# The first part's list of steps in another order, with the first step of 31 weight conversions on ScalarE

## The chip, the cores and the metric

The kernel runs on one core of a Trainium2 chip. The metric is the time of one execution on the device in microseconds (us); less is better. Before the change the median of 3 runs is 954.95 us (954.93 to 955.6).

The core's engines are TensorE (PE in the profile; PEld is its weight load), VectorE (DVE), ScalarE (ACT), GpSimd (POOL) and SyncE (SP), which issues all of this kernel's DMAs. Each engine takes its instructions in the order in which the program puts them. Semaphores between the engines follow from the data: an instruction waits for the last writer of what it reads and for the last readers of what it overwrites.

## The reference

Attention over q, k and v (4 batches, 8 heads, 576 positions, 64 channels), and then two pairs of dense layers over the 2304 tokens of 512 channels:

```python
# in each head; scale = 1/8, factor = 4
out_d     = softmax(scale * mean4(q) @ mean4(k).T) @ mean4(v)      # 144 pooled positions
out_local = softmax(mask(|i - j| < 4, scale * q @ k.T)) @ v        # a band of 7 keys
attn      = repeat(out_d, 4) + out_local
x  = attn as (2304, 512)
h  = x @ w_in;   x = (h * sigmoid(1.702 * h)) @ w_out              # first block, d_ff 2048
h  = x @ w_in2;  y = max(0.01 * h, h) @ w_out2                     # second block
```

The weights come as float64 and are turned into float32 pairs on the chip.

## The kernel before, in words

**Attention** is cut into 16 jobs, one for a batch and a pair of heads (128 channels). Job n's steps carry its number: loads q, k, va, vb, vh; sums over four positions Qd, Kd (VectorE), Va0 to Vb1 (POOL); pooled scores Sd (TensorE), their maximum Mxd (VectorE), exponentials Exd (ScalarE), inverse sums Rcd (VectorE), division Mud (POOL), transposes T0, T1 (TensorE) copied out by C0, C1 (ScalarE), and the product Vd copied out by Od. The band's scores S0 and S1 are for one head each; jobs 0 to 3 have the mask added by TensorE and go through M, N (VectorE) and E (ScalarE, one call for each of five slices), jobs 4 to 7 through A0, A1, Mx, Sb, Ex, Sm. Then Rc and Mu (division, POOL), transposes U0, U1 copied out by D0, D1, products Y0, Y1, and X0, X1, which add both results on VectorE and give x.

**The two blocks** run over 5 groups of columns (512, then four of 448 tokens) and 16 slices m of the 2048 hidden channels. A unit is one group and one slice. L is a unit's first product (12 matmuls into a PSUM bank h), M its second (12 matmuls into the four accumulators). In between stand Gt (ScalarE, out of h), Gd (VectorE), Gh (ScalarE, the rounded part) and Gl (POOL, what is left). Units 0 and 1 take their first product in pieces h0, h1 of 128 channels, after xh and xl have split x. The two banks of h are reused in turn, so L of a unit waits for Gd of the unit two before.

**Weights.** Slice m of the first block has two halves: number 2m (for L of unit m) and 2m + 1 (for M of unit m). w.n loads half n, 512 KB, into one of three stage buffers. Six steps convert it (`w_conv`, `w_bits`): wF scales the upper words of the doubles into t (line 175), wL shifts (177), wS adds the sign (180), wB adds the lower bits (184), wH rounds into the matmul's format (ScalarE, line 156) and wO subtracts to get the rest (POOL, line 203). The first four run on VectorE; there are three buffers for t. `copy` (lines 154 to 157) picks the engine of wF, wH and other copies: VectorE's form is on line 157, ScalarE's on line 156.

**The order.** The first part (jobs 0 to 7, the 32 conversions, units 0 to 13 of L and 0 to 11 of M) is written out by hand as the list ORDER, one token a step. The list is walked from left to right and each step's instructions are put at the end of their engines' queues: each engine has the list's order among its own steps, and the list fixes nothing between engines but by the data. `@V`, `@G` and `@A` put a step on VectorE, POOL or ScalarE instead of its usual engine. z tokens are matmuls on a constant, with no use of their result. t.23, t.25 and t.27 begin job 8. After the list a loop does the remaining units, jobs 8 to 15 and the second block's weights.

`w_slot` gives a slice m its space when its first half's conversion begins (line 198). The 16 such spaces are also what jobs 0 to 3 use for their tiles before.

Of the kernel before, what the change touches and what calls it, by code (L numbers as in the profile page):

```python
# [27 lines left out]
def attn_moe_kernel(ctx: ExitStack, tc, qT_d, kT_d, vh_d, vg_d, w1a, w2a, w1b, w2b, outT):  # L28
# [18 lines left out]
    ENGINES = {"V": V, "G": G, "A": nc.scalar}  # L47
    HEAD = 2
    ORDER = """
        q.0 vb.0 k.0 k.1 Qd.0 q.3 Vb0.0 va.0 Kd.0 q.1 Vb1.0 Kd.1 w.0 Qd.3 z3.12 S1.0 Va0.0 k.2 Va1.0  # L50
        Qd.1 vb.3 Sd.0 vb.1 M1.0 va.2 N1.0 va.5 E1.0 Mxd.0 vb.2 z3.3 S0.0 vh.0 Kd.2 Vb0.3 Exd.0 S1.1
        M0.0 q.2 Vb1.3 N0.0 Va0.2@V Vb0.1 E0.0 vh.1 Sd.1 M1.1 Va1.2 Rcd.0 va.3 Vb0.2 N1.1 Mud.0@V
        vb.4 E1.1 Mxd.1 Vb1.1 w.1 z3.2 T1.0 Vb1.2 T0.0 Rc.0 S0.1 Qd.2 Mu.0 C0.0 q.4 C1.0 Va0.3@V
        S1.2 Exd.1 M0.1 va.1 Vb0.4 Va0.5@V U0.0 N0.1 vh.2 M1.2 U1.0 Vb1.4 Rcd.1 D1.0 N1.2 wF.0 z3.2
        Vd.0 D0.0 w.2 Mud.1 E0.1 wF.1 Y1.0 wL.0 wL.1 Va0.1 T1.1 wS.0 Sd.2 k.3 Od.0 Va1.3 C1.1 Rc.1
        Va1.1 X1.0 va.4 S0.2 E1.2 Mu.1 Mxd.2 T0.1 k.4 M0.2 Y0.0 C0.1 N0.2 Qd.4 vh.3 E0.2 U1.1 Kd.3
        Va0.4 z3.1 Vd.1 vh.4 X0.0 U0.1 Va1.4 Exd.2 Rc.2 S0.3 vb.5 Od.1@V Mu.2 wB.0 D0.1 Rcd.2 z3.1
        S1.3 w.3 xh.0 M0.3 Mud.2 wH.0 wS.1 z3.1 Sd.3 D1.1 N0.3 M1.3 xl.0 E0.3 N1.3 wB.1 Y1.1 T0.2
        Vb0.5 X1.1 U1.2 E1.3 U0.2 C0.2@V wO.0 T1.2 Mxd.3 w.4 Y0.1 C1.2 Rc.3 Exd.3 wF.2 z3.1 h0.0
        Mu.3 X0.1 Vd.2 wL.2 D0.2 Rcd.3 wH.1 wS.2 z2.1 Y0.2 Mud.3 D1.2 Od.2 wB.2 xh.1 Y1.2 wO.1 X0.2  # L60
        w.5 wH.2 U0.3 Kd.4 U1.3 T0.3 wO.2 D1.3 X1.2 C0.3 wF.3 z3.1 T1.3 xh.2 wL.3 C1.3 wS.3 z3.1
        h1.0 xl.2@G D0.3 wF.4 Vd.3 wB.3 Y1.3 xl.1 wL.4 w.6 wH.3 Y0.3 Od.3@V wS.4 wO.3 h0.1 wB.4 X0.3
        h0.2 wH.4 wF.5 S0.4 X1.3 wO.4 wL.5 xh.3 S1.4 wS.5 w.7 xl.3 h1.1 wF.6 wL.6 h1.2 wB.5 q.5 h0.3
        wS.6 wH.5 k.5 h1.3 wB.6 Gt.0 wO.5 L.2 A1.4 wH.6 w.8 Gd.0 wO.6 wF.7 Gh.0 wL.7 wS.7 Gl.0 L.3
        A0.4 wB.7 Gt.1 Mx.4 w.9 wH.7 Gd.1 Sb.4 wF.8 Gh.1 M.0 wL.8 wO.7 wS.8 Ex.4 wB.8 Gl.1 Sm.4 w.10
        wH.8 Sd.4 wO.8@V Gt.2 Rc.4 M.1 Qd.5 Mu.4 Gd.2 wF.9 Gh.2 Kd.5 w.11 Gl.2 wL.9 L.4 wF.10 wS.9
        Gt.3 wL.10 wB.9 wS.10 wH.9 S1.5 wB.10 wO.9 w.12 M.2 A1.5 wH.10 Gd.3 wO.10 wF.11 Gh.3 wL.11
        Gl.3@V L.5 wS.11 Gt.4 w.13 Gd.4 wB.11 Gh.4 wF.12 wH.11 Gl.4 Mxd.4 M.3 wL.12 Exd.4 wO.11
        wS.12 w.14 wB.12 Gt.5 Gd.5 wH.12 S0.5 wF.13 Gh.5 wO.12 Rcd.4 U0.4 wL.13 q.6 M.4 A0.5 D0.4
        Mud.4 Mx.5 k.6 wF.14 w.15 Sb.5 wS.13 wB.13 T1.4 Gl.5 L.6 wL.14 C1.4 wS.14 wH.13 Ex.5 wB.14  # L70
        wO.13 Sm.5 wH.14 w.16 M.5 wO.14 Rc.5 Gt.6 wF.15 Gd.6 Mu.5 wL.15 Gh.6 wS.15 Gl.6 T0.4 wB.15
        w.17 Y0.4 C0.4 wF.16 wH.15 wL.16 Vd.4 wS.16 wO.15 L.7 Od.4@V wB.16 Va1.5 Vb1.5@V wH.16 X0.4
        va.6 wO.16@V vb.6 wF.17 Sd.5 Gt.7 w.18 wL.17 U1.4 Mxd.5 M.6 D1.4 Va0.6 Gd.7 Exd.5 Vb0.6 Qd.6
        Gh.7 Kd.6 Gl.7 Y1.4 Rcd.5 w.19 wF.18 S0.6 X1.4 wL.18 Mud.5 S1.6 wS.17 A0.6 M.7 q.7 wB.17
        A1.6 k.7 wH.17 wS.18 wO.17 w.20 Mx.6 T1.5 wB.18 U0.5 Sb.6 C1.5 vh.5 L.8 wF.19 D0.5 wL.19
        wH.18 wS.19 Ex.6 wO.18 wB.19 w.21 Sm.6 T0.5 Gt.8 Y0.5 wF.20 C0.5 wL.20 wH.19 Gd.8 Vd.5 wO.19
        wS.20 L.9 Gh.8 Od.5@V X0.5 w.22 Gl.8 wF.21 wL.21 wB.20 Va1.6 Sd.6 wS.21 Vb1.6 Gt.9 vb.7
        wH.20 va.7 Gd.9 U1.5 M.8 wO.20 Mxd.6 Gh.9 w.23 Kd.7 Exd.6 Gl.9 D1.5@V wB.21 Y1.5 Va0.7@V
        Vb0.7 wH.21 Rcd.6 S0.7 vh.6 X1.5 Mud.6 Rc.6 S1.7 A0.7 w.24 Mu.6 Qd.7 T1.6 M.9 A1.7 C1.6
        wO.21 wF.22 Mx.7 wL.22 Sb.7 wS.22 T0.6 wB.22 U0.6 Ex.7 L.10 wF.23 w.25 D0.6 wL.23 C0.6 Sm.7  # L80
        wH.22 Rc.7 wO.22 wS.23 Y0.6 Gt.10 wB.23 Mu.7 Gd.10 Vd.6 wH.23 w.26 wF.24 L.11 Gh.10 wO.23
        wL.24 Od.6 Vb1.7@V X0.6 wS.24 Gl.10 wB.24 U1.6 wF.25 Va1.7 Sd.7 Gt.11 D1.6@V w.27 wL.25
        wH.24 Gd.11 Y1.6 wO.24 M.10 Mxd.7 Gh.11 vh.7 wS.25 Exd.7 Gl.11 wB.25 Rcd.7 wH.25 w.28 wF.26
        Mud.7 U1.7 wL.26 M.11 D1.7 X1.6 wO.25 wS.26 wB.26 wF.27 wH.26 wL.27 T1.7 wO.26 w.29 wS.27
        T0.7 C1.7 L.12 C0.7 wB.27 wF.28 wH.27 wL.28 wO.27 wS.28 Vd.7 wB.28 Gt.12 w.30 U0.7 wF.29
        L.13 Od.7@V D0.7 Gd.12 wH.28 wL.29 Gh.12 wO.28@V Gl.12 wS.29 wB.29 Y0.7 w.31 Gt.13 wF.30 t.23
        Y1.7 wH.29 wL.30 Gd.13 wO.29 X0.7 Gh.13 wS.30 Gl.13 wB.30 X1.7 wH.30 wF.31 wL.31 wO.30 wS.31
# [834 lines left out]
```

## Time and profile before

| what | value |
|---|---|
| median of 3 runs | 954.95 us |
| the profiled execution | 953.42 us |
| its span, first to last instruction | 951.6 us |
| TensorE busy (share of the span) | 909.0 us (96%) |
| VectorE busy | 449.3 us (47%) |
| POOL busy | 375.6 us (39%) |
| ScalarE busy | 306.8 us (32%) |
| mean granted TensorE clock | 0.985 |

The profiled execution has 1.82 us around its span. Busy shares are means over stages with different limits, so the stretch 0 to 188.3 us, in which the list's VectorE steps run, is read by itself. In the list of groups a group's mean includes what its instructions waited while they were already on the engine.

### The profile page before, as it was taken

Reading aid. Unit: us, or ns where it says so; the run is one execution under the profiler, and the core shown is the slowest. Engines: PE = TensorE matmul, PEld = TensorE weight load, DVE = VectorE, ACT = ScalarE, POOL = GpSimd, SP = SyncE. Lnnn points to the kernel's source line nnn. Section 1 sums busy time; section 2 is a strip of 40 time slices with the busy share of each in tenths; the row PEclk is TensorE's granted clock in tenths of the full one; section 3 lists DMA queues with packets and bytes.
Section 4 is the critical chain, followed back from the end, with each engine's and each line's share of the span. In section 5 each row is a group of like instructions: output and inputs, shape, how many; then the busy total and the mean of one; then the engine's idle time right before and its main releaser. Section 6 shows DMA issues by size and latency. Waiting matters only on the chain.

```text
span 951.6 us, 14188 instructions
## 1 busy us (share of the span) xinstructions
PE 909.0 (96%) x5562; PEld 790.4 (83%) x5562; DVE 449.3 (47%) x748; ACT 306.8 (32%) x676; POOL 375.6 (39%) x350
## 2 busy tenths in 40 slices
...
DVE  5999999955545538988931311121121112112111
...
GB/s 269 125 153 129 111 166 126 114 134 157 127 141 150 140 186 174 231 230 191 220 205 111 155 78 0 1 10 75 1 1 78 1 1 77 1 1 39 1 1 39
DMA packets 51906, 98.67 MB, mean 104 GB/s; under 512 B 11648, under 2 KB 25984, under 8 KB 51840
## 3 DMA queue, kind: packets, MB, share of 16 engines
...
## 4 chain that ended last, share of the span: by engine, by line
PE 82%; DVE 14%; issue 2%; DMA 1%; SPq 1%; ACT 0%; DVEq 0%; ACTq 0%
PE h L734 39%; PE acc L779 39%; DVE t L180 3%; DVE t L177 2%; DVE t L184 2%; DVE t L157 2%; DMA a<-vg 1%; PE av L568 1%; PE avd L509 1%; DVE g L753 1%; PE scd L438 1%; PE sc L355 1%; DVE stat L389 0%; DVE xf L599 0%; DVE P L369 0%
## 5 line engine op out<-in xcount | busy, mean ns | idle before, releaser
L734 PE MATMUL h<-xh,w 128*128 128x448 f32 (+1 forms) x1280 | 402.6, 375 | 5.7 <-POOL w L203 3.0
L779 PE MATMUL acc<-gh,w 128*128 128x448 f32 (+1 forms) x1280 | 399.2, 373 | 0.6 <-DVE g L753 0.6
L764 POOL TENSOR_TENSOR gl<-g,gh 128x448 fp32r<-128x448 f32 (+1 forms) x159 | 190.8, 1200 | 482.5 <-ACT gh L156 471.6
L734 PEld LDWEIGHTS h<-xh,w 128*128 128x128 f32 x1280 | 241.6, 189 | 36.5 <-POOL w L203 3.9
L779 PEld LDWEIGHTS acc<-gh,w 128*128 128x128 f32 x1280 | 241.6, 189 | 28.4 <-ACT g L752 1.8
L734 PE MATMUL h<-xl,w 128*128 128x448 f32 (+1 forms) x640 | 238.2, 372 | 1.3 <-POOL xl L717 1.3
L779 PE MATMUL acc<-gl,w 128*128 128x448 f32 (+1 forms) x640 | 237.9, 372 | 0.2 <-POOL gl L764 0.2
L760 DVE TENSOR_TENSOR g<-g,h 128x448 f32<-128x448 f32 (+1 forms) x80 | 50.7, 634 | 319.3 <-ACT g L759 319.3
L156 ACT ACTIVATE gh<-g 128x448 fp32r<-128x448 f32 (+1 forms) x160 | 94.3, 589 | 126.1 <-DVE g L753 69.3
L734 PEld LDWEIGHTS h<-xl,w 128*128 128x128 f32 x640 | 121.1, 189 | 13.8 <-POOL xl L717 1.8
L779 PEld LDWEIGHTS acc<-gl,w 128*128 128x128 f32 x640 | 120.8, 189 | 13.1 <-POOL gl L764 0.8
L759 ACT ACTIVATE g<-h 128x448 f32<-128x448 f32 (+1 forms) x80 | 44.4, 555 | 224.8 <-PE h L734 224.5
L753 DVE SCALAR_TENSOR_TENSOR g<-g,h 128x448 f32<-128x448 f32 (+1 forms) x80 | 50.5, 631 | 128.7 <-ACT g L752 128.2
L752 ACT ACTIVATE g<-h 128x448 f32<-128x448 f32 (+1 forms) x80 | 44.3, 554 | 162.6 <-PE h L734 149.8
L180 DVE SCALAR_TENSOR_TENSOR t<-s,t 128x512 uint32<-128x512 uint32 x64 | 82.4, 1288 | 1.6
L203 POOL TENSOR_TENSOR w<-t,w 128x512 fp32r<-128x512 f32 x28 | 39.5, 1416 | 34.5 <-ACT w L156 34.5
L184 DVE SCALAR_TENSOR_TENSOR t<-s,t 128x512 uint32<-128x512 uint32 x64 | 51.3, 802 | 1.8
L241 POOL TENSOR_TENSOR w<-b,w 128x1024 fp32r<-128x1024 f32 x16 | 38.4, 2403 | 7.4 <-ACT w L240 7.4
L382 POOL TENSOR_TENSOR P<-P,stat 128x320 f32<-128x320 f32 (+1 forms) x40 | 33.9, 863 | 18.1 <-DVE stat L421 14.1
L177 DVE TENSOR_SCALAR t<-t 128x512 uint32<-128x512 uint32 x64 | 39.9, 625 | 1.7
L157 DVE TENSOR_SCALAR t<-s 128x512 f32<-128x512 f32 x64 | 36.1, 565 | 3.6 <-DMA s<-w1b 2.7
L156 ACT ACTIVATE w<-t 128x512 fp32r<-128x512 f32 x32 | 20.3, 634 | 50.4 <-DVE t L184 50.4
...
## 6 DMA issues: line engine op xcount, KB each, us to landing
s<-w1a SPq DMA_DIRECT2D x16, 512.0 KB, 3.7
s<-w2a SPq DMA_DIRECT2D x16, 512.0 KB, 3.9
s<-w1b SPq DMA_DIRECT2D x16, 512.0 KB, 4.0
s<-w2b SPq DMA_DIRECT2D x16, 512.0 KB, 4.2
...
b<-wd SPq DMA_DIRECT2D x16, 512.0 KB, 3.5
...
```

Of the source, the lines that this page charges most:

```text
L156: return nc.scalar.activation(out=out, in_=in_, func=AF.Copy, scale=scale)
L157: return nc.vector.tensor_scalar(out=out, in0=in_, scalar1=scale, scalar2=None, op0=ALU.mult)
L177: lambda: nc.vector.tensor_scalar(out=b, in0=b, scalar1=3, scalar2=None, op0=ALU.logical_shift_left),
L180: lambda: nc.vector.scalar_tensor_tensor(out=b, in0=bits[:, :, 1], scalar=0x80000000, in1=b, op0=ALU.bitwise_and, op1=ALU.bitwise_or,),
L184: lambda: nc.vector.scalar_tensor_tensor(out=b, in0=bits[:, :, 0], scalar=29, in1=b, op0=ALU.logical_shift_right, op1=ALU.bitwise_or,),
L734: nc.tensor.matmul(h, w[:, kc * P : (kc + 1) * P], xs[kc][part], start=kc == 0 and i == 0, stop=kc == KC - 1 and i == 2,)
L752: lambda: nc.scalar.activation(out=g, in_=h[:, :n], func=AF.Tanh, scale=0.5 * 1.702),
L753: lambda: nc.vector.scalar_tensor_tensor(out=g, in0=g, scalar=1.0, in1=h[:, :n], op0=ALU.add, op1=ALU.mult),
L759: lambda: nc.scalar.activation(out=g, in_=h[:, :n], func=AF.Copy, scale=0.01),
L760: lambda: nc.vector.tensor_tensor(out=g, in0=g, in1=h[:, :n], op=ALU.max),
L764: lambda: on(G).tensor_tensor(out=gl, in0=g, in1=gh.bitcast(F32), op=ALU.subtract),
L779: nc.tensor.matmul(acc[c][:, :n], w[:, cs], g, start=m == 0 and i == 0, stop=m == NM - 1 and i == 2)
```

## The change

ORDER is replaced as a whole. The new list has the same steps but for the z tokens (17 matmuls instead of 26). 31 of the 32 wF steps have `@A`: all but wF.4. Other marks differ: without `@V` now are Va0.2, Va0.3, Va0.5, Va0.7, Mud.0, C0.2, Od.1, Od.3, Od.4, Od.5, Od.7, Vb1.5, Vb1.7, D1.5, D1.6, wO.8, wO.16 and wO.28; with `@V` now are xl.3, Gl.0, Gl.1, Gl.2, Gl.7, wO.12, wO.13, wO.15, wO.17, wO.20, wO.25, Mu.7 and wH.29. The conversions come in the order 4, 0, 6, 1, 2, 3, 5, 8, 16 with 21, 12, 10 with 9, 7, 14, 20 with 18, 11 with 13, 15, 22, 17 with 19, 24, 26, 31, 28, 23, 25 with 30, 27, 29. Since a slice's second half can now come first, `w_slot` is called for whichever comes first. The diff, cut: the beginning of the new list, the stretch before and after M.0, its end, and the condition.

```diff
     ORDER = """
...
+        w.4 wF.4 wL.4 wS.4 wB.4 wH.4 vb.3 Vb0.3 q.0 Qd.0 k.0 Kd.0 z3.5 S0.0 S1.0 M1.0 N1.0 wO.4 E1.0 vb.4 Vb0.4
+        Vb1.4 M0.0 q.1 Qd.1 N0.0 w.0 wF.0@A E0.0 Sd.0 Mxd.0 Exd.0 wL.0 wS.0 vb.1 Vb0.1 k.1 z3.2 S1.1 M1.1 wB.0
...
+        Kd.3 w.5 va.3 w.3 vh.1 wH.6 Od.0 Exd.2 D1.0 C0.1 D1.1 z3.2 Y1.0 X1.0 E1.3 U0.1 D0.1 vh.4 Rcd.2 Va0.1
+        Va1.1 Vd.1 Sd.3 Mxd.3 Qd.5 S1.5 A1.5 Va0.2 E0.3 Rc.3 Va0.4 Mu.2 U0.2 D0.2 wF.2@A wH.1 wL.2 X0.0 wS.2
+        Va1.4 Exd.3 Rcd.3 z2.1 S0.5 A0.5 Mud.4 T0.4 C0.4 wO.6 wB.2 va.5 vb.5 vh.3 vh.2 w.8 Mud.2 T0.2 C0.2 Sb.4
+        Ex.4 Sm.4 Va1.2 T1.4 C1.4 T1.2 C1.2 U1.2 Y0.1 wF.3@A D1.2 Y1.1 Od.1 X1.1 wL.3 xh.0 X0.1 Mu.3 U0.3 D0.3
...
+        h1.2 L.3 h1.3 w.16 wF.16@A wL.16 wH.8 Gd.2 Gh.2 wS.16 wB.16 wB.21 w.12 vh.5 vb.6 wO.8 L.4 Gl.2@V wF.12@A
+        X0.4 w.10 wL.12 wH.21 wO.21 w.9 wH.16 Gt.1 Gd.1 wS.12 wB.12 wO.16 Gh.1 Gl.1@V M.0 M.1 M.2 X1.4 wF.10@A
+        wL.10 wH.12 wF.9@A wL.9 wS.10 wS.9 wB.10 wB.9 Gt.3 Gd.3 wO.12@V Sb.5 wH.10 wO.10 L.5 wH.9 Gh.3 Gl.3@V
+        w.7 wF.7@A wL.7 wS.7 Gt.4 Gd.4 Gh.4 wB.7 wH.7 wO.9 k.6 Kd.6 Gl.4 q.6 Qd.6 w.14 wF.14@A wL.14 S1.6 Gt.5
...
+        D0.6 Gd.12 Gh.12 Va1.6 Vd.6 Od.6 wB.23 Va0.7 wH.23 w.30 vh.6 Y0.6 w.25 X0.6 wO.28 Mu.7@V Gl.12 Y1.6 X1.6
+        M.10 Gt.13 wF.25@A wF.30@A Vb1.7 t.25 wL.25 wL.30 wS.25 Gd.13 U1.7 D1.7 wS.30 wB.25 wB.30 Mud.7 T1.7
+        C1.7 T0.7 U0.7 C0.7 Va1.7 Vd.7 vh.7 D0.7 Y0.7 w.27 w.29 Od.7 X0.7 Y1.7 wO.23 M.11 Gh.13 wH.25 wO.25@V
+        Gl.13 X1.7 wF.27@A wH.30 wL.27 wS.27 wB.27 wF.29@A wL.29 wO.30 wS.29 wB.29 wH.29@V wO.29 wH.27 wO.27
+        t.27
     """
...
         t, fs = w_bits(e, m, i)
-        if i == 0:
+        if (e, m) not in wt:
             w_slot(e, m)
```

## Rows read from the trace of the kernel before

**Rows 1.** The page's 40 slices of the span, VectorE's busy tenths.
```profile
DVE  5999999955545538988931311121121112112111
```
**Rows 2.** Busy time by stretch: us, then each engine's, granted clock, DMA share, GB/s.
```profile
0.00:20.00 20.00, 15.71 (x136) 9.21 (x138) 10.47 (x24) 9.60 (x47) 11.11 (x26) 0.83 0.91 260
...
40.00:188.30 148.30, 119.62 (x946) 90.08 (x945) 144.25 (x223) 56.10 (x128) 84.30 (x64) 0.93 0.42 133
0.00:188.30 188.30, 149.39 (x1286) 109.24 (x1287) 174.48 (x284) 77.06 (x232) 107.77 (x104) 0.93 0.49 150
188.30:951.60 763.30, 759.57 (x4277) 681.18 (x4275) 274.82 (x465) 229.77 (x444) 267.79 (x246) 1.00 0.29 92
```
**Rows 3.** The chain that ended last, 150 to 190 us: start, us, what.
```profile
150.61 0.84 PE av L568 x24
...
152.24 2.95 PE h L734 x12
...
182.85 0.28 DVE x L599
...
183.26 1.34 PE sc L355 x38
184.60 3.90 PE h L734 x12
```
**Rows 4.** Groups by shape, 0 to 188.3 us: busy us, mean ns | idle before.
```profile
L180 DVE SCALAR_TENSOR_TENSOR t<-s,t 128x512 uint32<-128x512 uint32 x32 | 41.3, 1290 | 0.5
L203 POOL TENSOR_TENSOR w<-t,w 128x512 fp32r<-128x512 f32 x28 | 39.5, 1416 | 34.5 <-ACT w L156 34.5
...
L184 DVE SCALAR_TENSOR_TENSOR t<-s,t 128x512 uint32<-128x512 uint32 x32 | 29.2, 911 | 0.7
...
L177 DVE TENSOR_SCALAR t<-t 128x512 uint32<-128x512 uint32 x32 | 23.7, 744 | 0.6
L156 ACT ACTIVATE w<-t 128x512 fp32r<-128x512 f32 x32 | 20.3, 634 | 50.4 <-DVE t L184 50.4
L157 DVE TENSOR_SCALAR t<-s 128x512 f32<-128x512 f32 x32 | 20.1, 630 | 0.0
...
L753 DVE SCALAR_TENSOR_TENSOR g<-g,h 128x512 f32<-128x512 f32 x14 | 9.5, 677 | 0.1
...
L752 ACT ACTIVATE g<-h 128x512 f32<-128x512 f32 x14 | 8.3, 592 | 12.4 <-POOL gl L764 8.7 <-PE h L734 2.0 <-DVE gl L764 1.8
...
L203 DVE TENSOR_TENSOR w<-t,w 128x512 fp32r<-128x512 f32 x4 | 2.7, 685 | 0.7 <-ACT w L156 0.7
```
**Rows 5.** Timeline, 165 to 176 us: conversions one behind the other (start, us).
```profile
168.16 1.30 POOL L203 TENSOR_TENSOR w<-t,w 128x512 fp32r<-128x512 f32 x1 [2.01 <-ACT w L156]
168.25 1.76 DVE L180 SCALAR_TENSOR_TENSOR t<-s,t 128x512 uint32<-128x512 uint32 x1
170.04 0.69 DVE L184 SCALAR_TENSOR_TENSOR t<-s,t 128x512 uint32<-128x512 uint32 x1
170.65 0.42 DVE L157 TENSOR_SCALAR t<-s 128x512 f32<-128x512 f32 x1
...
171.10 0.43 DVE L177 TENSOR_SCALAR t<-t 128x512 uint32<-128x512 uint32 x1
```
**Rows 6.** Timeline, 31 to 39.5 us: one VectorE instruction beside five of POOL.
```profile
32.23 1.26 POOL L382 TENSOR_TENSOR a<-a,stat 128x640 f32<-128x640 f32 x1
32.27 5.76 DVE L180 SCALAR_TENSOR_TENSOR t<-s,t 128x512 uint32<-128x512 uint32 x1
...
36.22 1.25 POOL L203 TENSOR_TENSOR w<-t,w 128x512 fp32r<-128x512 f32 x1
```
**Rows 7.** DMA issues by line: KB each, median us from issue to landing.
```profile
s<-w1a SPq DMA_DIRECT2D x16, 512.0 KB, 3.7
```
**Rows 8.** Timeline, the first 20 us: VectorE's first instruction, first reduction of scores.
```profile
3.77 0.75 DVE L329 TENSOR_REDUCE a<-a 128x144 f32<-128x576 f32 x1 [3.77 <-DMA a<-qT]
...
10.40 0.48 DVE L402 TENSOR_REDUCE stat<-sc 128x5 f32<-128x320 f32 x1
```

More of the change, by code (lines that the diff above doesn't have):

```diff
@@ L49, in attn_moe_kernel @@
     ORDER = """
[L50 to L87, printed above, removed]
@@ L88, in attn_moe_kernel @@
-        t.25 wB.31 wH.31 wO.31@V t.27
+        w.4 wF.4 wL.4 wS.4 wB.4 wH.4 vb.3 Vb0.3 q.0 Qd.0 k.0 Kd.0 z3.5 S0.0 S1.0 M1.0 N1.0 wO.4 E1.0 vb.4 Vb0.4
+        Vb1.4 M0.0 q.1 Qd.1 N0.0 w.0 wF.0@A E0.0 Sd.0 Mxd.0 Exd.0 wL.0 wS.0 vb.1 Vb0.1 k.1 z3.2 S1.1 M1.1 wB.0
+        N1.1 E1.1 S0.1 M0.1 Rcd.0 N0.1 Rc.0 vb.0 va.0 Vb0.0 Vb1.0 Vb1.1 wH.0 Kd.1 z3.4 Sd.1 q.4 Qd.4 q.2 vb.2
+        k.2 S1.2 k.4 S0.4 Mxd.1 E0.1 Rc.1 S1.4 Kd.4 M1.2 A1.4 Vb1.3 Kd.2 Exd.1 Rcd.1 q.3 w.6 wF.6@A N1.2 E1.2
+        w.2 Qd.2 wL.6 S0.2 M0.2 wS.6 N0.2 Va0.0 A0.4 wB.6 z3.1 Sd.4 Mxd.4 z3.2 Sd.2 Qd.3 Mud.0 T1.0 C1.0 T0.0
@@ new lines, in attn_moe_kernel @@
+        k.3 S1.3 E0.2 M1.3 Rc.2 va.4 va.2 va.1 Mu.0 U0.0 D0.0 wO.0 Mud.1 N1.3 C0.0 U1.0 S0.3 Mxd.2 M0.3 Exd.4
+        w.1 Va1.0 Vd.0 wF.1@A wL.1 T1.1 C1.1 Rcd.4 wS.1 T0.1 Mu.1 vh.0 Y0.0 U1.1 k.5 q.5 Vb0.2 Mx.4 wB.1 N0.3
+        Kd.3 w.5 va.3 w.3 vh.1 wH.6 Od.0 Exd.2 D1.0 C0.1 D1.1 z3.2 Y1.0 X1.0 E1.3 U0.1 D0.1 vh.4 Rcd.2 Va0.1
+        Va1.1 Vd.1 Sd.3 Mxd.3 Qd.5 S1.5 A1.5 Va0.2 E0.3 Rc.3 Va0.4 Mu.2 U0.2 D0.2 wF.2@A wH.1 wL.2 X0.0 wS.2
+        Va1.4 Exd.3 Rcd.3 z2.1 S0.5 A0.5 Mud.4 T0.4 C0.4 wO.6 wB.2 va.5 vb.5 vh.3 vh.2 w.8 Mud.2 T0.2 C0.2 Sb.4
@@ new lines, in attn_moe_kernel @@
+        Ex.4 Sm.4 Va1.2 T1.4 C1.4 T1.2 C1.2 U1.2 Y0.1 wF.3@A D1.2 Y1.1 Od.1 X1.1 wL.3 xh.0 X0.1 Mu.3 U0.3 D0.3
+        U1.3 D1.3 Rc.4 Va0.3 Kd.5 wS.3 wO.1 wH.2 Mud.3 T0.3 C0.3 Vb1.2 Vd.2 wF.5@A T1.3 C1.3 Od.2 Vd.4 Y0.2 X0.2
+        Y1.2 X1.2 xl.0 xh.1 Sd.5 wO.2 h1.0 wB.3 Mxd.5 wF.8@A wL.5 wL.8 Y1.3 Va1.3 xh.2 Vd.3 Od.4 Od.3 Y0.3 X0.3
+        h0.0 xl.1 h0.1 wH.3 Exd.5 Mu.4 U0.4 D0.4 U1.4 h1.1 D1.4 Y1.4 Y0.4 wS.5 X1.3 xh.3 wB.5 wH.5 xl.3@V wS.8
+        Rcd.5 wB.8 wO.3 xl.2@G h0.2 h0.3 Gt.0 Gd.0 Mx.5 Gh.0 Gl.0@V Mud.5 w.21 wF.21@A wL.21 wS.21 wO.5 L.2 Gt.2
```

11 lines of the change are left out of this document (added).

## The prediction

> **What bounds the kernel now.** I read the page's slices first, then the busy time by stretch, then the chain of waits, then groups of instructions. In the slices VectorE stands at 9 tenths from the second slice to the eighth and falls to 5 and below after [rows 1]. The stretches give the edge: until 188.3 us VectorE is busy for 174.48 us, and from 40 us on for 144.25 of 148.3 (97%), while ScalarE has 56.1 there and POOL 84.3; after 188.3 TensorE is busy for 759.57 of 763.30 us [rows 2]. So the run is two stages in a row: some 184 us in which VectorE sets the pace, and a dense TensorE stage of fixed length. The seam is on the chain: X1 of job 7 (an addition on VectorE) ends at 183.1, the next scores on TensorE wait for it, and from 184.60 TensorE doesn't stop [rows 3]. What the change is worth is by how much that addition comes earlier. TensorE's work behind it is the same.
>
> In the first stage the 32 weight conversions are the largest item: 0.630 + 0.744 + 1.290 + 0.911 = 3.575 us each on VectorE, 114.4 of the 174.5 us [rows 4]. These means are not the price of the instructions. Left alone, the first two take 0.42 and 0.43 us and the last 0.69; the third took 1.76 where a POOL subtraction of 1.30 had started 0.09 before it, and it ended 0.55 us after that one [rows 5]. At 32.27 the same form took 5.76 us, across several POOL instructions that followed each other from 32.23 to 37.47 [rows 6]. So VectorE waits for POOL in these forms: (0.630-0.42) + (0.744-0.43) + (1.290-0.69) + (0.911-0.69) = 1.34 us a conversion, 43 us in all (the third's undisturbed price is taken as the fourth's, the same form).
>
> **The change, part by part.**
>
> *31 first steps (all but that of conversion 4) go to ScalarE.* VectorE loses between 31 x 0.42 = 13.0 us and 31 x 0.630 = 19.5 us [rows 4, 5]. I take 13.0: POOL's subtractions are still there, and what the first step waited for them the second will likely wait for.
> The Trainium skill (SBUF - State Buffer, Who interferes with whom) says that a VectorE instruction in a two-port mode or with two SBUF inputs and a GpSimd instruction exclude each other for a whole instruction, and that ScalarE waits for nobody. The row of 5.76 us agrees. By that rule the saving is the undisturbed price, 13.0 us, and not the mean's 19.5.
>
> ScalarE gains 31 steps. It doesn't show this form; its nearest row, the rounding copy of the same tile, takes 0.634 us [rows 4], so some 19.7 us on top of 77 in 188 [rows 2]: half used. Its price lies between VectorE's undisturbed 0.42 (13 us) and, for the wider stride of the doubles' upper words, twice the row (1.27, 39 us); I take the row. Even the upper end leaves ScalarE under 120 of some 170 us, so its sum doesn't bind; its order may, which is the next term.
>
> *The wait it adds.* VectorE's second step now waits for ScalarE, whose queue is in order: ahead of the first step stand wH of earlier conversions, Gt (waits for TensorE) and Gh. Behind the waiting wL stand all of VectorE's steps. I walked one stretch by rows, each step starting when its engine and its inputs are free: 0.43 or 0.69 for VectorE's conversion steps [rows 5], 0.68 for Gd, wO and Gl there, 0.63 for ScalarE's copies and wF, 0.59 for Gt [rows 4]. Numbers are ends, with Gd.1's end as 0. VectorE: wS.12 0.69, wB.12 1.38, Gl.1 2.06, X1.4 2.4; ScalarE: Gh.1 0.63, wF.10 1.26, wH.12 (after wB.12) 2.01, wF.9 2.64. VectorE: wL.10 2.83, wL.9 3.26, then wS.10, wS.9, wB.10, wB.9 to 6.0; ScalarE: Gt.3 3.2. Gd.3 6.7, wO.12 7.4; ScalarE wH.10 5.9, wH.9 6.6, Gh.3 7.3, wF.7 8.0; VectorE Gl.3 8.1, wL.7 next. No stall, without POOL's delays, which give ScalarE more room. Likewise wF.14 is done at 11.9 where VectorE wants it at 12.0. Where Gt waits for TensorE (Gt.0, Gt.1) I find 0.3 to 0.5 us. A slot of the three stage buffers is refilled as soon as wB has read it, and a load lands 3.7 us after its issue [rows 7]; the tightest pair (wB.16 to wF.10, 4.5 us of VectorE's steps by the undisturbed prices) just covers 3.7 + 0.63. The price is 0 to 19 us (0 to 0.6 a conversion); I take 2.
>
> *Other steps that change engine.* 18 leave VectorE: three wO at 0.685 [rows 4] and fifteen smaller ones (Va0, Vb1, Od, D1, C0, Mud) at 0.42 to 0.685, 8.4 to 12.4 us. 13 come: six wO, four Gl, xl.3, Mu.7, wH.29, about 13 x 0.685 = 8.9. Net +0.5 to -3.5; I take -1. POOL loses twelve of some 1.41 us (17 us) and gains ten, most of them on smaller tiles (7 to 14 us): -3 to -10. VectorE waits 43 us for POOL's 107.8, 0.4 of it, so -1 to -4; I take -2.
>
> *The start.* In the first 20 us VectorE is busy for 10.47 [rows 2]; it starts at 3.77, when the first q lands [rows 8], and then waits for the next ones. Now a 512 KB weight goes first: at the stretch's 260 GB/s [rows 2] q.0 lands 2 us later, and VectorE has a conversion to do meanwhile (2.2 us undisturbed). M1.0 then needs only Qd.0 and Kd.0 ahead, against five such reductions now. Idle time falls or rises: -6 to +4, I take -2. Nine of 26 warming products of TensorE go; they lie beside these waits, and the granted clock is 0.83 with them [rows 2], so 0; with a lower clock only the small attention products would take longer there. The loads are the same ones in another order. SP takes them in order and stops at a weight until a stage buffer is free: w.3 waits for wB.1 and holds vh.1 and five more loads behind it, but vh.1 is used 63 steps later: 0 to 2, within the range above.
>
> *The seam.* Behind X1.7 now stand about 5 us of VectorE's list (183.1 to 188.3); in the new one two conversions without first step, 3.6 to 5.9, and wH.29. Ahead of it comes Qd of job 8 (0.74). Both ways under 1.5 us: 0. Nothing late replaces it: M.11 stands ahead of X1.7 in the new list and its conversion (23) is four ahead of the last, and M.13, which needs the last conversion, comes behind scores, L.14, M.12 and L.15, each unit 2.95 us or less [rows 3].
>
> **Sum.** -13.0 + 2 - 1 - 2 - 2 + 0 = -16.0 us on the profiled execution's 953.42: 937.4. The runs' median is 1.53 us above that execution, so 939.
>
> **Rivals.**
> A. *POOL holds VectorE longer.* In the new list eleven POOL steps (Va0.1 to Va1.2) stand close together around the conversions 2 and 6. Each wait such as the one at 32.27 costs 5.76 - 1.29 = 4.5 us [rows 4, 6]. One to three more of them leave a gain of 11.5 to 2.5, so 943 to 952, in the middle 948. For it: the row of 5.76, once. Against: POOL's sum falls.
> B. *The hand-over through ScalarE sets the pace (slower).* If wF regularly sits behind wH, Gt and Gh, 0.634 + 0.592 + 0.634 [rows 4], VectorE stands for up to 1.9 us in each of 31 conversions. It decides from (16 + 2)/31 = 0.58 us a conversion; at 1.0 the kernel takes 31 x 1.0 - 18 = 13 us more: 968. For it: today VectorE never waits inside a conversion (0.5 us in all before the 32 third steps) [rows 4], and the queue that is put between is shared with TensorE's results. Against: the walk above, and ScalarE's half-empty queue.
> C. *The change does nothing.* The 0.42 us freed is waited away for POOL, and the hand-over eats the rest: 955. For it: a conversion's four steps and POOL's one together, 2.2 + 1.3 us, stay near what a conversion takes now. Against: the 13.0 us are time in which VectorE worked, not time in which it waited for POOL.
> TensorE as the new bound I exclude as a cap above: from M.0 on the new list has 21 units, 62 us at 2.95, and some 5 us for each of three jobs (an av piece takes 0.84) [rows 3]; VectorE has 21 conversions at 2.945 (62 us) and the jobs' reductions besides.
>
> **Chances.** The forecast, gain of 8 to 24 us, 931 to 947: 0.62. A: 0.20, nearly all of it faster. C: 0.05. B: 0.13. So faster by over 0.2% (1.9 us, about what a measurement of this kernel can tell) 0.81, within 0.06, slower 0.13. The range takes the forecast's and A's: 930 to 951.
>
> **What would show it.** Right: VectorE's busy time to the seam near 155 to 160 us, some 13 to 20 less; L157 on t as 31 ScalarE instructions near 0.63; X1 of job 7 ending near 167; the dense TensorE stage as long as before. Each step wrong: waits of VectorE (L177) for ScalarE of over 10 us in sum speak for B; third steps of 3 us and more for A; a first reduction of scores later than the 10.40 us of now [rows 8], a worse start. The prediction is wrong if X1.7 ends after 176 us, or if the stage behind it changes its length by over 3 us.

## The result, and the profile after

The changed kernel takes 930.95 us (median of its runs, 930.12 to 931.21) against 954.94 for the kernel before beside it: the ratio is 0.9749, 95% interval 0.9732 to 0.9765. The gain is 24.0 us, where 16 were predicted. Lines from 90 on carry numbers four lower than before: wF's VectorE form is L153, wL L173, wS L176, wB L180, ScalarE's copies L152, wO L199.

First the page: busy time and share of the span by engine, VectorE's tenths in 40 slices (against [rows 1]), and the engines' shares of the chain that ended last.

```profile
PE 904.3 (97%) x5553; PEld 789.6 (85%) x5553; DVE 425.2 (46%) x712; ACT 324.1 (35%) x714; POOL 368.5 (40%) x348
...
DVE  6989999645455379888711311121121121112111
...
PE 87%; DVE 9%; issue 1%; ACT 1%; DMA 1%; POOL 0%; SPq 0%; ACTq 0%; DVEq 0%
```

The last of these lines in the kernel before:

```profile
PE 82%; DVE 14%; issue 2%; DMA 1%; SPq 1%; ACT 0%; DVEq 0%; ACTq 0%
```

The stretch of 8 and 9 tenths at the start ends one slice sooner. Next the busy time by stretch of the kernel after (columns as in [rows 2]):

```profile
0.00:20.00 20.00, 13.76 (x121) 8.01 (x121) 12.41 (x27) 10.78 (x52) 12.60 (x27) 0.91 0.94 302
40.00:160.10 120.10, 108.39 (x843) 84.09 (x842) 114.51 (x175) 67.99 (x149) 71.28 (x60) 0.94 0.48 153
0.00:160.10 160.10, 140.03 (x1222) 104.96 (x1223) 144.87 (x241) 92.91 (x268) 97.04 (x100) 0.93 0.55 174
160.10:928.30 768.20, 764.28 (x4333) 684.63 (x4331) 280.29 (x473) 231.15 (x446) 271.51 (x249) 1.00 0.29 92
```

and the kernel before up to the same event, the end of X1 of job 7:

```profile
0.00:183.11 183.11, 144.35 (x1236) 104.98 (x1236) 170.06 (x278) 76.13 (x231) 106.22 (x103) 0.93 0.50 153
```

That addition ends at 160.13 instead of 183.11 us, 23.0 earlier. What is behind it lasts 768.2 us against 951.6 - 183.1 = 768.5. So the whole gain lies in the first stage. VectorE is busy for 25.2 us less in it (170.06 - 144.87); it stands idle 2.2 us more (160.10 - 144.87 = 15.23 against 183.11 - 170.06 = 13.05).

The chain around the seam (start, us, what; [rows 3] before):

```profile
156.08 0.68 PE avd L505 x5
...
156.94 1.15 PE av L564 x37
158.09 2.95 PE acc L775 x12
161.03 0.74 PE sc L351 x40
161.78 2.95 PE h L730 x12
```

No addition on VectorE stands on it any more: TensorE's own queue (the last job's products, then the 12 matmuls of M.11, which end at 161.04) ends 0.9 us after X1.7. The first stage is now close to both limits.

The groups by shape of the first 160.1 us ([rows 4] before: busy us, mean ns, idle time before and its cause):

```profile
L199 POOL TENSOR_TENSOR w<-t,w 128x512 fp32r<-128x512 f32 x23 | 31.6, 1380 | 27.6 <-ACT w L152 27.4
L176 DVE SCALAR_TENSOR_TENSOR t<-s,t 128x512 uint32<-128x512 uint32 x30 | 30.7, 1025 | 0.5
L180 DVE SCALAR_TENSOR_TENSOR t<-s,t 128x512 uint32<-128x512 uint32 x30 | 28.1, 946 | 0.3
...
L173 DVE TENSOR_SCALAR t<-t 128x512 uint32<-128x512 uint32 x31 | 21.3, 697 | 0.3 <-ACT t L152 0.2
L152 ACT ACTIVATE t<-s 128x512 f32<-128x512 f32 x30 | 19.7, 666 | 3.1 <-DMA s<-w2a 1.5 <-DVE w L199 1.5 <-POOL w L199 0.2
...
L199 DVE TENSOR_TENSOR w<-t,w 128x512 fp32r<-128x512 f32 x7 | 8.3, 1180 | 0.1
```

The first steps stand on ScalarE, and VectorE waits 0.2 us in all for them. VectorE's other three steps fell too, wS most: 1290 ns in [rows 4], 1025 here.

One place in the timeline of the kernel after shows how that can come about (start, us):

```profile
65.12 0.69 DVE L749 SCALAR_TENSOR_TENSOR g<-g,h 128x512 f32<-128x512 f32 x1 [0.55 <-ACT g L748]
65.31 1.29 POOL L199 TENSOR_TENSOR w<-t,w 128x512 fp32r<-128x512 f32 x1
65.73 0.81 DVE L385 TENSOR_REDUCE stat<-P 128x10 f32<-128x640 f32 x1
...
66.51 0.69 DVE L760 TENSOR_TENSOR gl<-g,gh 128x512 fp32r<-128x512 f32 x1
67.12 0.42 DVE L173 TENSOR_SCALAR t<-t 128x512 uint32<-128x512 uint32 x1
```

A wO of 1.29 us runs beside a gate and a reduction, both at their usual price, and wL behind takes its undisturbed 0.42. In [rows 5] the same POOL instruction cost wS over a microsecond. Summed over the records, POOL and a conversion step ran at the same time for 69.7 us before and 46.7 after; these times hold the waits themselves. The waits in the 32 conversions (their durations less 0.42, 0.43, 0.69 and 0.69, as in the prediction) fell from 43.1 to 26.0 us, by 17.0 before rounding.

### The profile page after: what moved, and what is told of

Its sections match the earlier page's. It is cut to its first block, busy times and chain, and to the rows that moved or that the text cites. A ratio compares the mean times of both kernels' runs of the same rounds, so it can differ in the third digit from the quotient of the medians.

```text
span 928.3 us, 14196 instructions
## 1 busy us (share of the span) xinstructions
PE 904.3 (97%) x5553; PEld 789.6 (85%) x5553; DVE 425.2 (46%) x712; ACT 324.1 (35%) x714; POOL 368.5 (40%) x348
## 4 chain that ended last, share of the span: by engine, by line
PE 87%; DVE 9%; issue 1%; ACT 1%; DMA 1%; POOL 0%; SPq 0%; ACTq 0%; DVEq 0%
PE acc L775 40%; PE h L730 40%; PE av L564 2%; DVE t L176 2%; DVE t L180 1%; PE avd L505 1%; DVE t L173 1%; PE sc L351 1%; PE scd L434 1%; DVE g L749 1%; DMA a<-kT 1%; DVE w L199 1%; ACT a L407 0%; PE pdt L461 0%; DVE stat L385 0%
## 5 line engine op out<-in xcount | busy, mean ns | idle before, releaser
L760 POOL TENSOR_TENSOR gl<-g,gh 128x448 fp32r<-128x448 f32 (+1 forms) x155 | 184.8, 1192 | 483.1 <-ACT gh L152 469.7
L152 ACT ACTIVATE gh<-g 128x448 fp32r<-128x448 f32 (+1 forms) x160 | 94.2, 589 | 125.3 <-DVE g L749 68.8
L176 DVE SCALAR_TENSOR_TENSOR t<-s,t 128x512 uint32<-128x512 uint32 x64 | 73.2, 1144 | 1.7
L180 DVE SCALAR_TENSOR_TENSOR t<-s,t 128x512 uint32<-128x512 uint32 x64 | 51.6, 811 | 1.4
L199 POOL TENSOR_TENSOR w<-t,w 128x512 fp32r<-128x512 f32 x25 | 34.2, 1374 | 31.6 <-ACT w L152 27.4
L173 DVE TENSOR_SCALAR t<-t 128x512 uint32<-128x512 uint32 x64 | 38.8, 611 | 1.4 <-ACT t L152 0.2
L713 DVE TENSOR_TENSOR xl<-xf,xh 128x448 fp32r<-128x448 f32 (+1 forms) x25 | 19.2, 783 | 19.3 <-ACT xh L152 19.1
L152 ACT ACTIVATE w<-t 128x512 fp32r<-128x512 f32 x31 | 19.2, 628 | 24.2 <-DVE t L180 24.2
```

The lines of the kernel that those rows point to most:

```text
L173: lambda: nc.vector.tensor_scalar(out=b, in0=b, scalar1=3, scalar2=None, op0=ALU.logical_shift_left),
L176: lambda: nc.vector.scalar_tensor_tensor(out=b, in0=bits[:, :, 1], scalar=0x80000000, in1=b, op0=ALU.bitwise_and, op1=ALU.bitwise_or,),
L180: lambda: nc.vector.scalar_tensor_tensor(out=b, in0=bits[:, :, 0], scalar=29, in1=b, op0=ALU.logical_shift_right, op1=ALU.bitwise_or,),
L760: lambda: on(G).tensor_tensor(out=gl, in0=g, in1=gh.bitcast(F32), op=ALU.subtract),
```

## The experiments

Every time is a median beside runs of the kernel before on the same chip (954.7 to 955.1 there). The columns in between are from the profiled run, to the end of X1.7: VectorE's busy and idle time from the busy time by stretch. The waits are worked out as above and count all 32 conversions, of which one or two end behind X1.7. The profiled run needn't be the middle one: with the small scalings on ScalarE it was the fastest (931.49 us), with the 8 small adds back the slowest (937.25 us), so these two rows go with those times. "Marks" are the 31 `@` marks other than wF's that the change altered. Differences of 3 to 4 us to the kernel after are hardly told apart by these runs (its interval of the ratio ends at 0.9765, and those of 934 to 935 us begin near 0.975), though every run of these kernels was slower than every run of the kernel after (931.21 at most); those of 10 us and more are told apart.

| kernel | us | X1.7 ends | VectorE busy | idle | waits in conversions |
|---|---|---|---|---|---|
| before | 954.9 | 183.1 | 170.1 | 13.1 | 43.1 |
| after | 930.95 | 160.1 | 144.9 | 15.2 | 26.0 |
| new list and marks, wF on VectorE | 942.64 | 173.0 | 159.7 | 13.3 | 31.6 |
| old list and marks, wF on ScalarE | 946.57 | 173.9 | 152.4 | 21.5 | 33.8 |
| old list, new marks, wF on ScalarE | 948.09 | 177.2 | 149.3 | 27.9 | 28.1 |
| new list, old marks, wF on ScalarE | 949.4 | 178.0 | 147.7 | 30.2 | 28.5 |
| after, small scalings on ScalarE | 935.1 | 162.5 | 140.2 | 22.3 | 27.4 |
| after, all wO on VectorE | 941.51 | 168.9 | 144.4 | 24.5 | 12.0 |
| before, conversions in twos | 959.9 | 188.3 | 161.9 | 26.4 | 34.2 |
| old list, wF on ScalarE earlier | 948.32 | 176.8 | 156.5 | 20.3 | 35.7 |
| after, conversions one by one | 934.94 | 165.1 | 147.4 | 17.7 | 28.8 |
| after, 8 small adds back | 934.06 | 167.7 | 142.3 | 25.5 | 23.1 |
| after, 15 weight steps back | 945.25 | 174.0 | 140.4 | 33.6 | 25.9 |
| after, 8 evictions back | 934.19 | 162.9 | 145.3 | 17.6 | 23.6 |

**The order without the move.** The list of after with its 31 new marks, and all first steps on VectorE:

```diff
- w.10 wL.12 ... wF.10@A wL.10
+ w.10 wL.12 ... wF.10 wL.10
```

> The new list with all 32 first steps (wF) back on VectorE: the order alone. Theory O (the waits of VectorE for POOL shrank because the new list puts POOL's instructions beside steps that don't wait for them; the move gives only the undisturbed 0.42 us a step): 931 + 13 = 944 us, and the other three steps of a conversion keep near 2.62 us in mean (now 0.689 + 1.004 + 0.931). Theory M (they shrank because 31 instructions that can wait left VectorE, whatever the order): the three steps go back to near 2.95 us and wF waits as well, 953 to 961 us.

942.64 us, ratio 0.9869 (0.9853 to 0.9885): half of the gain. The groups of its first 173 us have the first step at

```profile
L153 DVE TENSOR_SCALAR t<-s 128x512 f32<-128x512 f32 x31 | 25.1, 813 | 4.9 <-DMA s<-w1a 4.9
L173 DVE TENSOR_SCALAR t<-t 128x512 uint32<-128x512 uint32 x30 | 20.8, 700 | 0.7
```

so 31 x (0.813 - 0.42) = 12.2 us of waits stood in the first steps here. The other three steps' means sum to 2.417 against 2.624 in the kernel after: taking the first steps away put 32 x 0.207 = 6.6 of those 12.2 us into the next ones, and the rest of them went away. The time is near theory O's 944; the three steps, with the first one back in front of them, are shorter than either theory said.

**The move without the order.** The list of before, the mark alone:

```diff
- wF.9 ... wF.10 ...
+ wF.9@A ... wF.10@A ...
```

> The old list with 31 wF (all but wF.4) on ScalarE: the move alone. Theory O: 955 - 13 = 942 us, the other three steps of a conversion stay near 2.95 us. Theory M: their mean falls to about 2.6 us, 925 to 932 us. A third one, hand-over: the old list has wF right before its wL, so VectorE waits for ScalarE's queue: idle time before wL (line 177) of 10 us or more, 945 to 960 us.

946.57 us, ratio 0.9905 (0.989 to 0.992). VectorE is busy for 17.7 us less, but its waits (us in all, times, longest) now have this line:

```profile
DVE t L177 <- ACT t L156: 9.0, 13, 2.0
```

Rival B's mechanism is there, at 9.0 us (to 180 us), in the list that wasn't made for the move; in the new one it is 0.2. The third theory, the hand-over, comes nearest: the other three steps' means sum to 2.834 us, between the 2.95 of theory O and the 2.6 of theory M.

**Less work on VectorE early on.** The kernel after, with N and the second operation of Mxd on ScalarE:

```diff
-            nc.vector.tensor_scalar(out=mx, in0=mx, scalar1=-SCALE, scalar2=None, op0=ALU.mult)
+            nc.scalar.activation(out=mx, in_=mx, func=AF.Copy, scale=-SCALE)
```

> The new list, and the eight N steps and the second instruction of the eight Mxd on ScalarE (16 tiny multiplications, 3.3 + 3.9 us of VectorE by their means, most of it waits for POOL; ScalarE gets 16 of some 0.2 us). If VectorE's sum to the seam sets the time: 931 - 4 to 7 = 924 to 927 us. Rival: where they stand VectorE waits for loads and ScalarE anyway, and a longer ScalarE queue delays E and Exd: 930 to 935 us.

935.1 us, ratio 0.9778 (0.9757 to 0.9798): no gain over the kernel after, rather a loss of up to 4 us. Between 20 and 60 us VectorE has less to do (columns as before; first the kernel after, then this one):

```profile
20.00:60.00 40.00, 35.04 (x477) 25.73 (x477) 35.34 (x72) 27.74 (x109) 26.73 (x27) 0.83 0.43 134
```

```profile
20.00:60.00 40.00, 33.89 (x442) 24.71 (x443) 29.81 (x60) 26.61 (x116) 25.61 (x26) 0.87 0.43 135
```

but it is idle for 10.2 us in place of 4.7. (Of the 12 instructions fewer, 9 are those that moved.) The step wB that starts at 55.47 us in the kernel after starts at 58.36 here. In this stretch the kernel after shows no wait of VectorE for ScalarE, and this one shows 6.7 us of them, the largest

```profile
DVE stat L416 <- ACT a L407: 3.5, 3, 1.7
```

There the chain through several engines sets the pace, not VectorE's sum, as the rival had it.

**POOL's subtractions taken away.** The kernel after with all 32 wO on VectorE:

```diff
- wO.4 ... wO.0 ...
+ wO.4@V ... wO.0@V ...
```

> The new list with all 32 wO on VectorE (25 more there, none on POOL). Theory P (VectorE's long conversion steps are waits for a POOL instruction in progress, 11.7 of the 26 us beside wO): 25 x 0.69 = 17 us more work, 10 to 14 us of waits less, the three other steps of a conversion fall from 2.62 to near 2.2 us: 934 to 939 us. Rival (the stretch has another cause, such as the load on the memory by all engines together): the steps stay near 2.62 us and the time rises by the full 17: 948 us.

941.51 us, ratio 0.9854 (0.9835 to 0.9874). The groups of the first 168.9 us:

```profile
L199 DVE TENSOR_TENSOR w<-t,w 128x512 fp32r<-128x512 f32 x29 | 26.3, 921 | 0.0
L180 DVE SCALAR_TENSOR_TENSOR t<-s,t 128x512 uint32<-128x512 uint32 x30 | 24.3, 822 | 0.3
L176 DVE SCALAR_TENSOR_TENSOR t<-s,t 128x512 uint32<-128x512 uint32 x30 | 23.8, 798 | 0.5
...
L173 DVE TENSOR_SCALAR t<-t 128x512 uint32<-128x512 uint32 x31 | 17.9, 585 | 1.0 <-ACT t L152 0.9
```

With POOL's wO gone the three steps fall toward their undisturbed prices (2.184 us in sum, as theory P said) and the waits by 14.0 to 12.0 us. So it is POOL that lengthens them. The time lies between the two theories: the 25 more wO cost VectorE as much as that saves (144.4 us busy against 144.9), and the kernel is slower by its idle time, 24.5 us in place of 15.2. The largest part of it is behind TensorE's products, where the kernel after waits 3.5 us:

```profile
DVE xf L595 <- PE av L564: 9.4, 6, 5.9
```

**Conversions in twos, in the old list.**

```diff
- wF.8 ... wL.8 ... wS.8 ... wB.8 ... wF.9 ... wL.9 wS.9 ...
+ wF.8 wF.9 ... wL.8 wL.9 ... wS.8 wS.9 ... wB.8 wB.9 ...
```

> The list of before, all of the first steps (wF) on VectorE as there; only conversions 8 to 31 are put in twos, step beside step (wF.8 wF.9 ... wL.8 wL.9 ... wS.8 wS.9 ... wB.8 wB.9); nothing else moves. In the trace of before the late conversions wait for GpSimd in a chain, 28.5 us in the last 24, and 21 of 27 of GpSimd's subtractions wO lie over 0.5 us beside a conversion; in the list of after 10 of 23 do. Theory I (standing in twos is what lets the wO by): about a third of the late waits goes, some 9 us, time 946 (942 to 950). Rival J (it is where the whole list puts other VectorE steps beside GpSimd's work, not the twos): waits stay within 3 us of 43.1 in all, time 953 to 957.

The waits fell by 8.9 us, as theory I had it, and the kernel became slower: 959.9 us, ratio 1.0038 (1.0018 to 1.0058). Both theories missed the time. VectorE is busy for 8.2 us less and idle for 13.4 more. In the waits to 188.3 us stands a new line, about half of that, and two loads lie on the chain:

```profile
DVE t L152 <- DMA s<-w2a: 6.5, 4, 2.6
```

```profile
171.92 3.45 DMA s<-w2a
...
178.40 3.77 DMA s<-w2a
```

That fits three stage buffers which two conversions in step empty two at a time and late, so that the next load is waited for; no run with more buffers shows it.

**The first step earlier in the old list.**

```diff
- wL.8 wO.7 wS.8 ... wB.8 ... wF.9@A ... wL.9
+ wF.9@A wL.8 wO.7 wS.8 ... wB.8 ... wL.9
```

> The list of before with 31 first steps on ScalarE, as in the run with the move alone (946.57 us), but each of them stands one conversion earlier in the list, in front of the second step of the conversion before, so that ScalarE has it sooner in its queue. With the move alone VectorE waited 9.0 us for ScalarE's copies (13 times, 2.0 us the longest). Theory H (the place in ScalarE's queue makes that wait): it falls under 2 us and the time to 939 to 942. Rival K (VectorE then only waits for GpSimd or TensorE instead, or ScalarE's other steps come late behind the copies): 945 to 949.

The wait for ScalarE goes as theory H expected,

```profile
DVE t L173 <- ACT t L152: 1.1, 1, 1.1
```

but the time doesn't (948.32 us, as rival K expected). Idle time fell by only 1.2 us, and VectorE's busy time rose by 4.1, of which 1.9 are waits for POOL. The wait that was removed by itself was paid elsewhere.

**Conversions one by one in the new list.** The mirror of the twos:

```diff
- wL.9 wS.10 wS.9 wB.10 wB.9
+ wS.10 wB.10 wL.9 wS.9 wB.9
```

> The list of after, but where it runs two conversions step beside step (8 places, 32 of VectorE's 96 conversion steps) they are put one after the other in the same places of the list. Mirror of the twos in the list of before. Theory I (the twos save waits): 4 to 8 us more, 935 to 939. Rival J (the twos are by the way): 930 to 932.5, waits of the conversions within 2 us of 26.0.

934.94 us (ratio 0.9774, 0.9752 to 0.9796): 4.0 more, at the low edge of theory I (935 to 939). Waits are 2.8 us up and idle time 2.5. (In the pair 18 and 20 the places keep their engines, so the `@V` of wO.20 goes to wO.18.)

**The old marks in the new list.**

```diff
- Mud.0 ... C0.2 ... xl.3@V ... Gl.0@V ... wO.8 ...
+ Mud.0@V ... C0.2@V ... xl.3 ... Gl.0 ... wO.8@V ...
```

> The list of after with the first steps on ScalarE, but all 31 other engine marks that the change altered put back (7 subtractions wO on VectorE become 4, 5 Gl there become 1, Va, Vb, Od, D, C as before). The prediction gave these trades -1 us, bounds +0.5 and -3.5. Theory T (the trades are small, the order does it): 930 to 934. Rival U (the marks belong to the list: with three more wO and four more Gl on GpSimd the waits of conversions come back, at about 0.57 us of wait for each us of GpSimd beside them): 4 to 7 us more of wait, partly paid by 7 fewer steps of 0.7 to 1.2 us on VectorE, time 935 to 940.

949.4 us, ratio 0.993 (0.9912 to 0.9948). Neither T nor U: 18.4 us. VectorE is busy only 2.8 us more and its waits for POOL are up 2.5, but it is idle for 15.0 more, in lines such as

```profile
DVE stat L398 <- PE sc L351: 6.8, 4, 3.2
DVE g L749 <- ACT g L748: 4.9, 4, 3.3
...
DVE xf L595 <- ACT a L407: 3.1, 1, 3.1
DVE t L173 <- ACT t L152: 3.0, 4, 1.9
```

**Three groups of these marks by themselves.**

```diff
- Mud.0 Va0.2 Va0.3 Va0.5 Va0.7 Vb1.5 Vb1.7 Mu.7@V
+ Mud.0@V Va0.2@V Va0.3@V Va0.5@V Va0.7@V Vb1.5@V Vb1.7@V Mu.7
```

> With all 31 old engine marks back (the first steps staying on ScalarE) the list of after took 949.4 us in place of 930.95, so the marks that were priced at -1 us are worth some 18 us in that list. Which of them? Here 8 small ones only: the additions Mud.0, Va0.2, Va0.3, Va0.5, Va0.7, Vb1.5, Vb1.7 back on VectorE, Mu.7 back on GpSimd. In the run with all marks the first 7 us of the lag came between 30 and 38 us, where VectorE waited 4.6 us for TensorE's scores, in the stretch of Mud.0, C0.2, Va0.3 and Od.1. Theory T1 (each mark costs its own few tenths on VectorE and no more): 931 to 933. Theory T2 (an early step on VectorE late makes a queue of waits across engines): 934 to 938.

934.06 us, 3.1 more, at T2's lower edge, and VectorE's waits for scores are up as T2 has it: 7.1 us, 1.6 in the kernel after (in the slowest of its five runs, the profiled one).

```diff
- xl.3@V Gl.0@V Gl.1@V Gl.2@V Gl.7@V wO.12@V wO.13@V ... wO.8 wO.16 wO.28 wH.29@V
+ xl.3 Gl.0 Gl.1 Gl.2 Gl.7 wO.12 wO.13 ... wO.8@V wO.16@V wO.28@V wH.29
```

> The list of after with 15 marks of before on weight and hidden-layer steps: xl.3, Gl.0, Gl.1, Gl.2, Gl.7, wO.12, 13, 15, 17, 20, 25 back on GpSimd, wO.8, 16, 28 on VectorE, wH.29 on ScalarE. With all marks back the lag grew from 8 to 16 us between 64 and 80 us, in the stretch of xl.3, Gl.0, Gl.2 and wO.8. Theory T1 (GpSimd's eight more instructions cost VectorE 0.57 us per us beside conversions and save 8 steps of 0.7 to 1.2 us there): 930 to 933. Theory T2 (GpSimd as the bound in that stretch: TensorE waits for gl and xl, hence VectorE later): 937 to 942.

945.25 us, 14.3 more, beyond T2's upper end. More than a quarter of it comes at one place, in the timeline of this kernel:

```profile
62.66 0.63 ACT L151 ACTIVATE xh<-xf 128x512 fp32r<-128x512 f32 x1
...
63.37 1.50 POOL L712 TENSOR_TENSOR xl<-xf,xh 128x512 fp32r<-128x512 f32 x1 [4.75 <-ACT xh L151]
64.82 1.26 POOL L198 TENSOR_TENSOR w<-t,w 128x512 fp32r<-128x512 f32 x1
66.04 1.26 POOL L712 TENSOR_TENSOR xl<-xf,xh 128x512 fp32r<-128x512 f32 x1
...
67.36 0.79 PE L729 MATMUL h<-xl,w 128*128 128x512 f32 x1 [2.73 <-POOL xl L712]
...
69.90 0.60 ACT L747 ACTIVATE g<-h 128x512 f32<-128x512 f32 x1 [6.08 <-PE h L729]
...
70.53 0.69 DVE L748 SCALAR_TENSOR_TENSOR g<-g,h 128x512 f32<-128x512 f32 x1 [6.79 <-ACT g L747]
```

POOL stands for 4.75 us in front of xl.3, which needs xh.3, and wO.3 and xl.2 are behind it in the queue; TensorE waits for the last, ScalarE for TensorE, and VectorE stands 6.79 us in front of Gd.0, with the next conversions behind it in its queue. In the kernel after VectorE takes xl.3 itself, for 0.68 us, POOL does xl.2 earlier, TensorE goes on at 63.13, and Gd.0 starts at 65.12, 5.4 us earlier:

```profile
60.22 1.74 POOL L713 TENSOR_TENSOR xl<-xf,xh 128x512 fp32r<-128x512 f32 x1
...
61.32 0.63 ACT L152 ACTIVATE xh<-xf 128x512 fp32r<-128x512 f32 x1
...
62.43 0.68 DVE L713 TENSOR_TENSOR xl<-xf,xh 128x512 fp32r<-128x512 f32 x1
...
63.13 0.39 PE L730 MATMUL h<-xl,w 128*128 128x512 f32 x1
```

xl.3 is the first of the 15 in the list, and xh.3 in front of it is already 1.3 us later here than in the kernel after; that part isn't due to these marks. The mark on xl.3 is worth the other 4.1 us.

```diff
- C0.2 Od.1 Od.3 Od.4 Od.5 Od.7 D1.5 D1.6
+ C0.2@V Od.1@V Od.3@V Od.4@V Od.5@V Od.7@V D1.5@V D1.6@V
```

> The list of after with 8 evictions of TensorE's sums (C0.2, Od.1, Od.3, Od.4, Od.5, Od.7, D1.5, D1.6) back on VectorE as before, where they take 0.2 to 0.4 us each and stand in its queue in the order of the list, so that what is behind them waits for TensorE. Theory T1 (their own 2 to 3 us): 932 to 935. Theory T2 (the waits for TensorE that VectorE's queue then has in it): 936 to 942. If the three groups sum to much less than 18 us, the marks only cost together.

934.19 us, 3.2 more: the time of T1, though not only by their own price, since VectorE's busy time is up 0.4 us (its waits for POOL are down 2.5) and its idle time 2.4. The three groups, 3.1 + 14.3 + 3.2 = 20.6, sum to about the 18.4 of all together, the two small ones being hardly told from nothing.

**The new marks in the old list.**

```diff
- Mud.0@V ... C0.2@V ... xl.3 ... Gl.0 ... wO.8@V ... wF.9
+ Mud.0 ... C0.2 ... xl.3@V ... Gl.0@V ... wO.8 ... wF.9@A
```

> The other way round: the list of before with every engine mark of after, the 31 first steps on ScalarE and the 31 others. With the 31 first steps alone it was 946.57 us. Theory T3 (the marks are good by themselves, some 18 us as in the new list): below 938. Theory T4 (the marks fit only the list they stand in; in the old list they are worth about what the prediction said, -1): 944 to 947, and then the order itself, with equal engines, is worth 13 to 16 us.

948.09 us, ratio 0.9916 (0.9889 to 0.9942): T4, a microsecond above its range. With the first steps moved, the marks cost 1.5 us in the old list (948.09 - 946.57) and give 18.4 in the new one (949.4 - 930.95). The list with the old marks costs 2.8 (949.4 - 946.57) and with the new ones gives 17.1 (948.09 - 930.95). The intervals of these three ratios overlap, so the two costs are not told from nothing; with the first steps moved, neither the new list nor the new marks gain anything without the other. What either does with the first steps on VectorE was not run.

## Why the prediction was right, and where its size was off

The sign, the place and the limit were right: the gain is an earlier end of VectorE's stage, X1.7 moves by 23.0 us, and the dense stage keeps its length within 0.3 us. The size was 8 us short: X1.7 ends at 160.1 where 167 was expected, VectorE is busy for 144.9 us where 155 to 160 were, and 930.95 us lies 0.95 inside the lower end of the range. That it lies inside is partly luck: the waits for POOL fell by 14 us more than forecast, and VectorE's other work and its idle time gave back 8.5 of that; without this the time would be near 922, outside the range. Term by term, to X1.7:

- *31 first steps, -13.0.* They stand on ScalarE with a mean of 0.666 us, near the row that was taken (0.634). What the rows don't give is how much of the first steps' waits passes on: "what the first step waited for them the second will likely wait for" held for 6.6 of 12.2 us in the new list. In the old one the waits fell from 43.1 to 33.8 us with the move, by 9.2, more than the first steps' own 6.7, so that there none was seen to pass on. The runs give the move 8.4 us in the old list (954.94 - 946.57) and 11.7 in the new one (942.64 - 930.95), against -13.0 + 2 = -11.
- *Hand-over, +2.* 0.2 in the new list. The walk by rows was right for it; in the old list it is 9.0 us over 31 conversions, 0.29 each, half of the 0.58 from which rival B decides.
- *Fewer POOL steps, -2: the term that was mis-sized.* Waits in the conversions fell by 17.0 us, 16.1 of it up to X1.7 (42.1 to 26.0). The prediction scaled them with POOL's sum (97 after, 106 before). They don't go by that sum. What fell with them is the time side by side with conversions, 46.7 us against 69.7. That time holds the waits themselves, so it describes more than it explains, but the count of POOL's wO that lie over 0.5 us beside a conversion fell too (of those that start before X1.7 ends, 21 of 27 to 11 of 23; the expectation of the twos has 10). The Trainium skill (SBUF - State Buffer, Who interferes with whom) has the rule behind it, that certain VectorE instructions and POOL's exclude each other; the run with all wO on VectorE agrees (three steps 2.184 us in place of 2.624). The prediction used the rule for the price of the moved step and, in rival A, for eleven POOL steps that might do harm, and did not ask beside which VectorE steps the other POOL instructions of the new list would fall. The new list and marks without the move take 11.5 us of waits away, the move alone 9.2, all together 17.0.
- *Other steps that change engine, -1.* The first steps (13.0 us), the waits (16.1) and conversion steps that now stand behind X1.7 (1.4) make 30.5 us less; VectorE's busy time fell by 25.2, so its other work rose by 5.3. The steps that came cost more than the 0.685 us of the prediction: seven wO took 1180 ns each, where four took 685 [rows 4], +5.6 by themselves. But the prediction priced a mark by its duration, and the runs show that this isn't what it is worth. Put back, the marks change VectorE's busy time by 2.8 us and the total by 18.4, through idle time. The mark on xl.3 is an example: 0.68 us on VectorE, and Gd.0 stands some 4 us earlier.
- *Start, -2.* VectorE is busy for 12.41 of the first 20 us, not 10.47 [rows 2]: 1.9 more, so the start went as forecast. The first reduction of scores comes at 10.41 as before [rows 8]. Later idle time took it back, so that it is +2.2 in all up to X1.7; the sum had no term for idle time behind the start but the hand-over.

In sum -13.0 - 16.1 - 1.4 + 5.3 + 2.2 = -23.0. Rival A didn't come: the mean of wS is 1.0 us and the longest 1.8. The cap that the prediction excluded, TensorE, is reached: its queue ends 0.9 us after X1.7.

The table also shows the limit of the waits as an explanation. With the twos in the old list they fell by 8.9 us and the kernel got slower; with the small adds back they are lower than in the kernel after (23.1) and the time is 3.1 longer. Busy time that is saved counts only if the other engines have VectorE's next step ready. Of the 23.0 us up to X1.7, 25.2 are busy time and -2.2 idle time; the three kernels that have the move with at most one of list and marks save 17.7 to 22.3 us of busy time and lose 8.4 to 17.2 of it to idle time. Why the new list and marks together avoid that is shown at one place, xl.3; for the other marks and for each move of the list, the nine z matmuls less among them, it stays open.
